# The column stage of a spectral filter beside a gated MLP: the column transform's step is dealt first in every gap, in ten gaps with three rests

## The chip, the cores and the metric

One core of a Trainium2 chip runs the whole kernel. The metric is the device time of one execution in microseconds (us); the kernel before takes 1312.53 us, the median of three runs (1312.05 to 1313.11). The core's engines are named as in its profile: PE is the matrix engine (PEld its weight loads), DVE the vector engine, ACT the scalar engine, POOL and SP mostly issue DMAs. Each takes its own instructions in the order in which the program lists them.

## The reference, cut to what matters

```python
def _A_ref(x, w_r, w_i):                       # x: 1 x 2048 x 576, float32
    X = jnp.fft.rfft2(x, axes=(-2, -1))
    X = X * (w_r + 1j * w_i)
    return jnp.fft.irfft2(X, s=(S, D), axes=(-2, -1))
def _B_ref(x, w_gate, w_up, w_down):           # 576 -> 4608 -> 576
    g, u = x @ w_gate, x @ w_up
    return (gelu(g) * u) @ w_down
g = sigmoid((x * gate_w).sum(-1, keepdims=True))
return g * _A_ref(A_x, A_w_r, A_w_i) + (1 - g) * _B_ref(A_x, w_gate, w_up, w_down)
```

Both branches read the same 2048 x 576 input.

## The kernel before, in words

**The MLP is PE's work and sets the order.** Float32 products are made of fp32r high and low parts. After two ordinary blocks the hidden layer is computed in 34 *groups* (`products`), each one a Strassen-like product of two hidden tiles and two blocks of 512 tokens: seven block products named a11, a12, s2, s3, s1, a22 and s4, each made of two *sevens* (`Block.seven`: seven 128x512 matmuls, lines 1399 and 1401, into the PSUM buffers `px` or `pgu`). Behind each pair of sevens stands a *down* (`down`, line 978: twelve 128x288 matmuls of the down projection into one of two `pdn` buffers); behind the last pair stand two. So a group has 14 sevens and 8 downs. Between them the other engines prepare weights (`Block.prep`: ACT copies the high part, DVE takes the low part, line 1383, and a DMA brings the tail, line 1375), copy PSUM tiles out, apply the GELU and multiply.

**Gaps.** Behind each seven and each down stands a *gap* (`gap`, `dealt`), 22 in a group. There the program first lists what is due by count (`at(n, fn)`: n gaps later), and then takes instructions from the spectral branch, a chain of Python generators in `gens`. A generator's `yield c` says that it has listed c us of DVE work; `yield None` ends its share of this gap. A number `credit` is raised by each matmul's time and lowered by DVE work; it is capped (`cap`, 2.4 in the column stage), and the generators are asked for more only while it is above zero.

**The spectral branch** runs on DVE, ACT and DMA beside the MLP: row transforms, then the *column stage* (`columns`), then the inverse row transforms. The column stage has two chains:

- The *column transform*: 16 steps `kb`. A step makes a first product from `xh`, `xl` (`product(0, ...)`, line 351: six 128x290 matmuls into a `pdn` buffer), copies it out (`zr`, `t0`), combines it on DVE (lines 432 and 433), turns it by two half copies on ACT (`turned`, lines 250 and 251), multiplies by the filter's weights `w0`, `w1` (lines 443, 444), adds (450 to 452) and splits the sum into a high part `yh` and a low part `yl` (431), from which the next step makes the second product, for column kb - 1; that one is copied back to a tile in `rows`. `xl` for the next step is line 457. The weights of the next step come by DMA on SP (line 341).
- The *chain beside it* (`beside`, held in `side`): butterflies and twiddles over four tiles (`column_four`, lines 259 and 266; `column_twiddles`, line 283), stores of finished tiles to `home` and loads of new ones from `away` (line 308, on SP). A backward part waits until the transform has four new tiles (`done`), the transform waits for a forward part (`made`).

In the kernel before, `dealt` asks the chain beside first while `ahead` is set, and then, if credit is left, the transform. A step takes at least eight gaps and more where the credit was used up. A down's result is copied out by ACT (line 1011) in the gap behind it (`post`).

Two PSUM buffers `pdn` serve downs and column products in turn, so a product or a down must wait until the one before the last has been copied out.

Of the kernel before, what the change touches and what calls it, by code (L numbers as in the profile page):

```python
# [27 lines left out]
ROWS = 5120  # L28
UNIT = ROWS // 4
RATE = 1.08  # L30
STEP = 8
FIRST = 2
APART = (13, 14, 16, 17)
PAIRS = ((2, 3, 4, 5), (6, 7, 8, 9), (10, 11, 12, 13), (14, 15, 16, 17), (0, 1))
# [126 lines left out]
def _build(nc, tc, a):  # L161
    with ExitStack() as ctx:
# [8 lines left out]
        def f(x):  # L171
            return x.bitcast(F32)
# [62 lines left out]
        def copy(o, i):  # L235
            act.activation(o, i, AF.Copy)  # L236
# [6 lines left out]
        def two(x):  # L243
            return x.rearrange("p (c k) -> p c k", c=2)[:, :, 0:NK]
# [3 lines left out]
        def turned(o, x, s):  # L248

            act.activation(o[0:64], x[64:128], AF.Copy, scale=-s)  # L250
            act.activation(o[64:128], x[0:64], AF.Copy, scale=s)
# [38 lines left out]
        def columns():  # L290
# [9 lines left out]
            def tile_of(kb):  # L300
                return G[kb // 4 % 2][kb % 4]
# [37 lines left out]
            def load_ww(kb, c):  # L339
                if kb < 16:  # L340
                    nc.sync.dma_start((w0, w1)[c], a["wf"][turn[kb], c])

            def step(us=0.0):
                credit[0] -= us
                yield None

            def product(d, kb, h, l):
                v = ps_dn()
                for al in range(2):
                    for n, (q, x) in enumerate(((0, h), (1, h), (0, l))):  # L350
                        pe.matmul(v[:, al, :NK], cc[d][2 * al + q], two(x)[:, al], start=n == 0, stop=n == 2)  # L351
                tick(6 * 0.135)
                at(1, lambda: load_cc(d, kb + 1))
                return v
# [66 lines left out]
            for kb in range(16):  # L421
                was, more = kb > 0, kb + 1 < 16
                v = product(0, kb, xh, xl)
                if was:
                    copy(yh, vs)
                yield from step()
                copy(zr, v[:, 1, :NK])
                copy(t0, v[:, 0, :NK])
                yield from step()
                if was:  # L430
                    vec.tensor_tensor(yl, vs, f(yh), ALU.subtract)
                vec.tensor_tensor(zi, t0, zr, ALU.subtract)
                vec.tensor_tensor(zr, t0, zr, ALU.add)
                yield from step(1.67 if was else 0.91)
                while post:
                    post.pop(0)()
                turned(vs, z, 1.0)
                u = product(1, kb - 1, yh, yl) if was else None
                yield from step()
                if was:  # L440
                    copy(two(tile_of(kb - 1)), u[:, :, :NK])
                    done[0] = kb - 1
                vec.tensor_tensor(z, z, w0, ALU.mult)
                vec.tensor_tensor(vs, vs, w1, ALU.mult)
                yield from step(1.52)
                if more:
                    while made[0] < (kb + 1) // 4:
                        yield None
                    copy(xh, tile_of(kb + 1))
                vec.tensor_tensor(z, z, vs, ALU.add)  # L450
                vec.tensor_tensor(vs2[:, 0], zr, zi, ALU.add)
                vec.tensor_tensor(vs2[:, 1], zr, zi, ALU.subtract)
                at(1, lambda kb=kb: load_ww(kb + 1, 0))
                at(2, lambda kb=kb: load_ww(kb + 1, 1))
                yield from step(1.67)
                if more:
                    vec.tensor_tensor(xl, tile_of(kb + 1), f(xh), ALU.subtract)
                yield from step(0.76)
                yield from waits(STEP - 7)
            copy(yh, vs)  # L460
            yield None
            vec.tensor_tensor(yl, vs, f(yh), ALU.subtract)
# [133 lines left out]
        def waits(n):  # L596
            for _ in range(n):
                yield None
# [145 lines left out]
        def spectral():  # L744
            nc.sync.dma_start(free_low[:, SW:SW + D], a["gw"][0:1, :].to_broadcast([P, D]))
            yield from send_away(0, lambda: load_rows(1))
            yield from waits(3)
            yield from other_gates()
            yield from forward_rows()
            yield from send_away(1, other_quads)  # L750
            stage_two = columns()
            ops["go"] = lambda: next(stage_two)
            yield from other_operands()
            yield from stage_two
            for h in range(2):
                yield from inverse_rows(h)
# [7 lines left out]
        gens = []  # L764
        side = []
        credit = [0.0]
# [7 lines left out]
        def at(n, fn):  # L774

            if n == 0:
                fn()
                return
            later.append((count[0] + n, fn))
            later.sort(key=lambda x: x[0])  # L780

        def gap():

            dealt()
            while post:
                post.pop(0)()

        def dealt():

            count[0] += 1  # L790
            while later and later[0][0] <= count[0]:
                later.pop(0)[1]()
            if aux:
                aux.pop(0)()
            credit[0] = min(credit[0], cap[0])
            if not gens:
                return
            ahead = side and ops.get("ahead")
            while ahead and credit[0] > 0:
                v = next(side[0], None)  # L800
                if v is None:
                    break
                credit[0] -= v
            while credit[0] > 0:
                try:
                    v = next(gens[0])
                except StopIteration:
                    gens.pop(0)
                    v = None
                if v is None:  # L810
                    while side and not ahead and credit[0] > 0:
                        v = next(side[0], None)
                        if v is None:
                            break
                        credit[0] -= v
                    return
                credit[0] -= v
# [247 lines left out]
        ops = {}  # L1065
# [201 lines left out]
        def tail_piece(n, raw_t=raw_t, high_t=high_t):  # L1267

            def load():
                for q, o in enumerate((raw_t[:, 0:2], raw_t[:, 3:7:3])):  # L1270
                    nc.sync.dma_start(o, a["wt"][n // 2, n % 2, q].rearrange("p (b k) -> p b k", b=2))

            def total():
                for o, p, q in ((4, 3, 0), (2, 6, 4), (3, 6, 3), (5, 1, 2)):
                    vec.tensor_tensor(raw_t[:, o], raw_t[:, p], raw_t[:, q], ALU.subtract)
                credit[0] -= 1.15

            def high():
                copy(high_t, raw_t)

            def rest():
                vec.tensor_tensor(fr(raw_t), raw_t, f(high_t), ALU.subtract)
                credit[0] -= 1.1

            def store():
                d = tails_d[n // 2].rearrange("(r p) (m c k) -> r p c m k", r=4, m=7, c=2)
                for r, x in enumerate((f(high_t), raw_t, f(high_t), raw_t)):
                    nc.sync.dma_start(d[r, :, n % 2], x)
                stored[n // 2] = n % 2

            return load, total, high, rest, store
# [116 lines left out]
        def products(b, k):  # L1408
# [4 lines left out]
            made = {}  # L1413
            opening, end, turn = k == 0, k == len(b.groups) - 1, (p, i) == (0, NBLK - 1)
            if opening:
                at(6, lambda: credit.__setitem__(0, credit[0] - 2.0))
                for q in range(2 * len(PAIRS) - 2):
                    t = (free_low[:, 0:7 * P] if q % 2 == 0 else wtb[:, 0:7 * P]).rearrange("p (m k) -> p m k", m=7)
                    for n, fn in zip((-4, 6, 8, 9, 10), tail_piece(q + 2, t)):
                        at(max(1, n + 12 * q), fn)  # L1420
# [219 lines left out]
        for k in range(len(b.groups)):  # L1640
            if k == len(b.groups) - 1:
                assert ops["half"]
            products(b, k)
# [63 lines left out]
```

## Time and profile before

| | |
|---|---|
| median of three runs | 1312.53 us (1312.05 to 1313.11) |
| profiled execution | 1312.65 us |
| its span | 1310.9 us |
| matmuls on PE, weight loads | 7210, 7210 |
| DVE, ACT, POOL busy share | 87%, 63%, 23% |
| first and last column product begin (us of the span) | 558.2, 855.5 |
| column products (six matmuls each) | 32 |
| DMA moved | 285.94 MB |

A time inside the span is counted from the span's start. [...] In a timeline row, `x6` merges six instructions that follow each other, and the bracket at the end gives the engine's idle time before the row and what ended it.

### The profile page before, as it was taken

What the parts mean: (1) busy time and instruction counts of PE and PEld (TensorE: products, weight loads), DVE (VectorE), ACT (ScalarE), POOL (GpSimd) and SP (SyncE); (2) the same over time, 40 slices, a digit from 0 to 9 for tenths busy, and PEclk for the clock granted to TensorE, in tenths of its full rate; (3) what the DMA queues carried; (4) which work ended last, traced back from release to release, by engine and by line L of the source; (5) the groups of instructions that cost most, each with busy time, mean ns of one, the idle gap of its engine ahead of it and who ended that gap; (6) DMA issues with size and microseconds to landing.
All of it is one profiled execution on the core that took longest, in us unless ns stands there. A gap on an engine that the chain in (4) does not pass through costs nothing.

```text
span 1310.9 us, 20543 instructions
## 1 busy us (share of the span) xinstructions
PE 1299.9 (99%) x7210; PEld 1150.1 (88%) x7210; DVE 1134.5 (87%) x1734; ACT 831.6 (63%) x1405; POOL 307.7 (23%) x392
## 2 busy tenths in 40 slices
PE   9999999999999999999999999999999999999998
PEld 7888888888888888888888888888888888888888
DVE  7899999988999998778888878778999977999954
ACT  5665655657565667678687878766555566565552
POOL 0011212122221211124321333333331231212151
PEclk9999999999999999999999999999999999999999
DMA  9779999897777799969988999999997798877797
GB/s 350 240 204 235 263 257 244 190 286 138 138 145 146 143 320 367 296 174 272 398 250 202 217 258 222 252 224 209 176 184 152 140 217 206 182 158 141 150 188 194
DMA packets 202537, 285.94 MB, mean 218 GB/s; under 512 B 18177, under 2 KB 118657, under 8 KB 201665
## 3 DMA queue, kind: packets, MB, share of 16 engines
q0 software_dynamic: 64848, 110.13, 49.4%
q1 hardware_dynamic: 137152, 174.06, 40.9%
q8 instruction: 56, 0.92, 0.3%
q10 hardware_dynamic: 432, 0.44, 0.1%
q14 instruction: 49, 0.39, 0.1%
HBM read 157.87 MB, written 137.88 MB: 226 GB/s over the span
## 4 chain that ended last, share of the span: by engine, by line
PE 86%; DMA 5%; DVE 4%; ACT 3%; issue 1%; SPq 1%; DVEq 0%; ACTq 0%
PE pdn L978 31%; PE px L1399 22%; PE pgu L1399 22%; PE px L1401 4%; PE pgu L1401 4%; DMA gub<-tails 1%; PE pdn L351 1%; DMA ye<-stg 1%; DMA gub<-ws 1%; DMA home<-rows 1%; ACT gub L236 0%; DMA tmp<-rows 0%; ACT stg L1011 0%; DMA low<-wgu 0%; DVE gub L1383 0%
## 5 line engine op out<-in xcount | busy, mean ns | idle before, releaser
L1011 ACT ACTIVATE stg<-pdn,omg 128x576 f32<-128x576 f32 x276 | 204.6, 741 | 328.8 <-PE pdn L978 182.5
L993 POOL DMA_DIRECT2D yd<-stg x232 | 202.1, 871 | 778.4 <-ACT stg L1011 752.6
L978 PE MATMUL pdn<-dn,hb 128*128 128x288 f32 x1356 | 199.9, 294 | 1.6 <-ACT rows L236 1.4
L978 PEld LDWEIGHTS pdn<-dn,hb 128*128 128x128 f32 x1356 | 191.7, 188 | 10.7 <-ACT rows L236 2.1
L1399 PE MATMUL pgu<-xhi,gub 128*128 128x512 f32 x480 | 149.0, 392 | 0.0
L1399 PE MATMUL pgu<-til,gub 128*128 128x512 f32 x516 | 132.1, 391 | 1.0 <-ACT xraw L236 1.0
L978 PEld LDWEIGHTS pdn<-dn,ext 128*128 128x128 f32 x816 | 122.2, 188 | 9.3
L978 PE MATMUL pdn<-dn,ext 128*128 128x288 f32 x816 | 129.3, 294 | 0.0
L978 PE MATMUL pdn<-dn,gub 128*128 128x288 f32 x816 | 129.3, 294 | 0.0
L1383 DVE TENSOR_TENSOR gub<-low,gub 128x512 fp32r<-128x512 f32 x151 | 103.4, 685 | 17.5 <-ACT gub L236 15.6
L978 PEld LDWEIGHTS pdn<-dn,gub 128*128 128x128 f32 x816 | 115.4, 188 | 0.0
L1399 PEld LDWEIGHTS pgu<-til,gub 128*128 128x128 f32 x516 | 94.4, 188 | 19.1 <-ACT xraw L236 1.2
L236 ACT ACTIVATE gub<-low 128x512 fp32r<-128x512 f32 (+1 forms) x163 | 100.7, 619 | 12.3 <-DMA low<-wgu 6.1
L1399 PE MATMUL px<-xhi,gub 128*128 128x512 f32 x344 | 106.9, 392 | 1.2 <-DVE gl L1427 0.7
L1399 PE MATMUL px<-til,gub 128*128 128x512 f32 x396 | 101.2, 391 | 0.0
L1399 PEld LDWEIGHTS pgu<-xhi,gub 128*128 128x128 f32 x480 | 86.6, 188 | 14.6
L1399 PE MATMUL pgu<-xlo,gub 128*128 128x512 f32 x240 | 93.6, 390 | 0.0
L1399 PEld LDWEIGHTS px<-til,gub 128*128 128x128 f32 x396 | 72.5, 188 | 13.7
L1399 PEld LDWEIGHTS px<-xhi,gub 128*128 128x128 f32 x344 | 62.0, 188 | 12.3 <-DVE gl L1427 1.2
L978 PE MATMUL pdn<-dn,hx 128*128 128x288 f32 x444 | 70.3, 294 | 0.0
L1401 PE MATMUL pgu<-til,gub 128*128 128x512 f32 x172 | 67.1, 390 | 0.4 <-DMA gub<-tails 0.4
L1399 PE MATMUL px<-xlo,gub 128*128 128x512 f32 x172 | 67.1, 390 | 0.0
(311 smaller groups left out, 2758.6 us busy)
## 6 DMA issues: line engine op xcount, KB each, us to landing
yd<-stg POOLq DMA_DIRECT2D x232, 288.0 KB, 5.4
low<-ws SPq DMA_DIRECT2D x114, 256.0 KB, 5.4
gub<-tails SPq DMA_DIRECT2D x179, 128.0 KB, 4.9
gub<-wd SPq DMA_DIRECT2D x68, 288.0 KB, 5.4
tails<-wtb SPq DMA_DIRECT2D x28, 448.0 KB, 5.6
ye<-stg POOLq DMA_DIRECT2D x32, 288.0 KB, 5.5
yd<-ye POOLq DMA_DIRECT2D x32, 288.0 KB, 7.4
slot<-tails SPq DMA_DIRECT2D x59, 128.0 KB, 4.6
```

Of the source, the lines that this page charges most:

```text
L236: act.activation(o, i, AF.Copy)
L351: pe.matmul(v[:, al, :NK], cc[d][2 * al + q], two(x)[:, al], start=n == 0, stop=n == 2)
L978: pe.matmul(ps[half], h[:, l, c], d[:, q, half * HD:(half + 1) * HD], start=part == 0 and n == 0, stop=part == 1 and n == 2)
L993: pl.dma_start(yd[u], o, accum_op=ALU.add)
L1011: out = lambda: put(u, lambda o: act.activation(o.rearrange("p (c k) -> p c k", c=2), v[:, :, 0:HD], AF.Copy, scale=omg[:, u:u + 1]), i == ...
L1383: vec.tensor_tensor(v[:, 0:5:4], x, f(v[:, 1:4:2]), ALU.subtract)
L1399: pe.matmul(ps, l, x[:, t], start=first and t == 0 and q == 0, stop=False, skip_group_check=True)
L1401: pe.matmul(ps, w[:, 512 + P * s:512 + P * (s + 1)], xt, start=False, stop=True, skip_group_check=True)
```

## The change

In `dealt`, while `ahead` is set and the chain beside is alive, the transform is asked for exactly one share in each gap, whatever the credit; the chain beside is then asked while credit is above zero, and nothing else happens in that gap. A step gets three rests (`yield None`): between the butterfly and the half copies with the second product, between that product's copy and the weight multiplications, and at the end, where it had one before. A step therefore has ten gaps. And in the first group a second debit of 1.5 us of credit is taken, four gaps behind the one of 2.0 us. No instruction of an engine's arithmetic is added or removed, apart from how repeated copies merge; what changes is where each stands among the others.

```diff
-STEP = 8
@@ columns
                 yield from step(1.67 if was else 0.91)
+                yield None
                 while post:
                     post.pop(0)()
                 turned(vs, z, 1.0)
                 u = product(1, kb - 1, yh, yl) if was else None
                 yield from step()
                 if was:
                     copy(two(tile_of(kb - 1)), u[:, :, :NK])
                     done[0] = kb - 1
+                yield None
                 vec.tensor_tensor(z, z, w0, ALU.mult)
...
                     vec.tensor_tensor(xl, tile_of(kb + 1), f(xh), ALU.subtract)
                 yield from step(0.76)
-                yield from waits(STEP - 7)
+                yield None
@@ dealt
-            ahead = side and ops.get("ahead")
-            while ahead and credit[0] > 0:
-                v = next(side[0], None)
-                if v is None:
-                    break
-                credit[0] -= v
+            if side and ops.get("ahead"):
+                credit[0] -= next(gens[0]) or 0.0
+                while side and credit[0] > 0:
+                    v = next(side[0], None)
+                    if v is None:
+                        break
+                    credit[0] -= v
+                return
             while credit[0] > 0:
...
-                    while side and not ahead and credit[0] > 0:
+                    while side and credit[0] > 0:
@@ products
             if opening:
-                at(6, lambda: credit.__setitem__(0, credit[0] - 2.0))
+                for n, us in ((6, 2.0), (10, 1.5)):
+                    at(n, lambda us=us: credit.__setitem__(0, credit[0] - us))
```

Where things stand now is told by the order of the instructions. In the kernel after the change a line that is compared has moved by one to four numbers (978 is 981, 351 is 350, 431 to 433 are 430 to 432, 443 and 444 are 444 and 445, 457 is 458, 963 is 966).

On PE, at the sixth second product (the one for column 5, made in the seventh step); before, it stands behind the last seven of a group:

```order
L1401 MATMUL pgu<-xtl_68,gub_73 128x512
L351 MATMUL pdn<-tmp 128x290 x3
L351 MATMUL pdn<-tmp,gub_73 128x290 x3
L978 MATMUL pdn<-dn,hb_79 128x288 x6
L978 MATMUL pdn<-dn,hx 128x288 x6
L978 MATMUL pdn<-dn,hb_79 128x288 x6
L978 MATMUL pdn<-dn,hx 128x288 x6
L1399 MATMUL px_6401<-xhi_63,slot 128x512 x2
```

and with the change the sixth second product stands behind the first pair of sevens of the next group:

```order
L1404 MATMUL px_6380<-til_334,slot 128x512
L350 MATMUL pdn<-tmp 128x290 x3
L350 MATMUL pdn<-tmp,gub_73 128x290 x3
L981 MATMUL pdn<-dn,hb_79 128x288 x6
L981 MATMUL pdn<-dn,hx 128x288 x6
L1402 MATMUL px_6379<-xhi_63,gub_72 128x512 x2
```

Behind the product there was a down and then another down; now there is one down and then a seven.

On DVE, at the butterfly of the eleventh step (`yl`, `zi` and `zr`, whose `wtb` is what ACT turns); this step's second product keeps its place on PE in front of two downs. Before:

```order
L1364 TENSOR_TENSOR low<-low 128x512
L1383 TENSOR_TENSOR gub_73<-gub_822,gub_73 128x2x256
L1427 TENSOR_TENSOR gl_82<-gl_82,px_6775 128x512
L431 TENSOR_TENSOR tmp<-wtb,tmp 128x580
L432 TENSOR_TENSOR wtb<-rows,wtb 128x290
L433 TENSOR_TENSOR wtb<-rows,wtb 128x290
L1368 TENSOR_TENSOR low<-low 128x512
```

and with the change:

```order
L430 TENSOR_TENSOR tmp<-wtb,tmp 128x580
L431 TENSOR_TENSOR wtb<-rows,wtb 128x290
L432 TENSOR_TENSOR wtb<-rows,wtb 128x290
L1367 TENSOR_TENSOR low<-low 128x512
L1386 TENSOR_TENSOR gub_73<-gub_822,gub_73 128x2x256
L1431 TENSOR_TENSOR gl_82<-gl_82,px_6764 128x512
L1371 TENSOR_TENSOR low<-low 128x512
```

Three instructions of the MLP that stood ahead of the butterfly now stand behind it.

On DVE, from the weight multiplications of the thirteenth step to the low part `xl` for the fourteenth; before:

```order
L443 TENSOR_TENSOR wtb<-wtb 128x580
L444 TENSOR_TENSOR wtb<-wtb,gub_822 128x580
L1383 TENSOR_TENSOR gub_73<-low,gub_73 128x2x256
L1364 TENSOR_TENSOR gub_822<-low,gub_822 128x512
L450 TENSOR_TENSOR wtb<-wtb 128x580
L451 TENSOR_TENSOR wtb<-wtb 128x290
L452 TENSOR_TENSOR wtb<-wtb 128x290
L963 TENSOR_TENSOR ext<-gl_82,ext 128x512
L1427 TENSOR_TENSOR xraw<-xraw 128x512
L259 TENSOR_TENSOR low<-rows 128x580
L259 TENSOR_TENSOR rows<-rows 128x580 x3
L457 TENSOR_TENSOR tmp<-rows,tmp 128x580
```

and with the change, from the addition of a seven ahead of them:

```order
L1448 TENSOR_TENSOR xraw<-xraw,px_7376 128x512
L444 TENSOR_TENSOR wtb<-wtb 128x580
L445 TENSOR_TENSOR wtb<-wtb,gub_822 128x580
L258 TENSOR_TENSOR low<-rows 128x580
L258 TENSOR_TENSOR rows<-rows 128x580 x3
L1448 TENSOR_TENSOR xraw<-xraw,px_7377 128x512
L451 TENSOR_TENSOR wtb<-wtb 128x580
L452 TENSOR_TENSOR wtb<-wtb 128x290
L453 TENSOR_TENSOR wtb<-wtb 128x290
L966 TENSOR_TENSOR gub_73<-xraw,gub_73 128x512
L458 TENSOR_TENSOR tmp<-rows,tmp 128x580
```

The four additions of `column_four` (line 259 before, 258 now) stood behind the three additions of the step (450 to 452) and now stand ahead of them, directly behind the weight multiplications. In the fifth and the ninth step they moved in the same way. On PE the first product that uses this `xl` stood ten gaps behind the second product of the thirteenth step, and now stands six gaps behind it, as in every step. The order also shows that the stage's last product stands one gap earlier than before, the first three gaps later, and that the debit in the first group leaves DVE's first 109 rows as they were; behind these, some instructions of the row transforms stand a gap or more later.

## The prediction

> **What bounds the kernel now.** First the page's head and its table of engines, for what is busy all the time:
>
> ```profile
> span 1310.9 us, 20543 instructions
> PE 1299.9 (99%) x7210; PEld 1150.1 (88%) x7210; DVE 1134.5 (87%) x1734; ACT 831.6 (63%) x1405; POOL 307.7 (23%) x392
> ```
>
> PE is busy for all but 11 us, and the change neither adds nor removes a matmul: it can only win back time in which PE was held up. So the next view is the table of windows, over the column stage and over one group behind it (the columns are busy times of PE, PEld, DVE, ACT and POOL, then granted clock, DMA share and GB/s):
>
> ```profile
> 553.57:937.21 383.64, 379.24 (x2135) 336.38 (x2134) 314.65 (x495) 282.19 (x472) 121.06 (x165) 1.00 0.98 240
> 937.21:972.22 35.01, 35.01 (x196) 31.02 (x196) 34.87 (x43) 18.85 (x31) 11.22 (x12) 1.00 1.03 183
> ```
>
> The windows are cut where the same down of a group begins: ten groups, then one. The undisturbed group takes 35.01 us (196 matmuls, 22 blocks, so 1.59 a block) at a granted clock of 1.00 in both. Ten such groups are 350.1; the first window has 2135 − 1960 = 175 more matmul records, of the column products' 192. A product runs .80 from start to start where nothing holds it up (783.13 to 783.93, below), so 32 are 25.6. 383.64 − 350.1 − 25.6 = **7.9 us lost** in the stage and just behind it. That is about all the change can win there. The view of waits, PE alone over that window, names some of it (us in total, times, longest):
>
> ```profile
> PE pdn L978 <- ACT rows L236: 1.4, 3, 0.5
> PE pgu L1399 <- ACT xraw L236: 1.0, 1, 1.0
> PE px L1399 <- DVE gl L1427: 0.7, 1, 0.7
> PE px L1399 <- ACT pgu L236: 0.5, 1, 0.5
> PE pgu L1401 <- DMA gub<-tails: 0.4, 1, 0.4
> PE pdn L351 <- DVE tmp L457: 0.2, 1, 0.2
> ```
>
> **What the change removes.** The timeline about one of the three waits for `rows`:
>
> ```profile
> 745.97 0.46 DVE L433 TENSOR_TENSOR wtb<-rows,wtb 128x290 f32<-128x290 f32 x1
> 746.52 0.69 ACT L250 ACTIVATE wtb<-wtb 64x580 f32<-64x580 f32 x1 [2.17 <-DVE wtb L433]
> 747.70 0.95 PE L978 MATMUL pdn<-dn,hx 128*128 128x288 f32 x6
> 748.48 0.64 ACT L236 ACTIVATE rows<-pdn 128x580 f32<-128x580 f32 x1
> 749.16 1.06 PE L978 MATMUL pdn<-dn,hb 128*128 128x288 f32 x6 [0.51 <-ACT rows L236]
> ```
>
> The second product (L351, just ahead on PE) stood before two downs. The second down needs the product's PSUM buffer; ACT copies it out only behind the half copies, and these wait 2.17 for the butterfly. From 747.70 to 749.16 are 1.46 where six matmuls take .79 (787.12 to 788.70 for twelve, below), so .67 lost, and .11 more as the restarted six last 1.06 instead of .95: the bracket and .27. The view of waits has three of them, 1.4 together: 1.4 + 3 × .27 = **2.2**. In the new order two of the three steps have one down and then a seven behind the product. The third, the eleventh step, keeps its place, but its butterfly stands ahead of three MLP instructions (.60 each from start to start): 1.8 earlier covers a wait of .5. I take all 2.2.
>
> A product between two downs costs less:
>
> ```profile
> 783.13 0.96 PE L351 MATMUL pdn<-tmp,xtl 128*128 128x290 f32 x6
> 787.12 1.74 PE L978 MATMUL pdn<-dn,hb 128*128 128x288 f32 x12
> 789.10 0.57 PE L351 MATMUL pdn<-tmp,gub 128*128 128x290 f32 x3
> 789.74 1.86 PE L978 MATMUL pdn<-dn,hb 128*128 128x288 f32 x12
> 631.92 0.57 PE L351 MATMUL pdn<-tmp,gub 128*128 128x290 f32 x3
> 632.56 1.73 PE L978 MATMUL pdn<-dn,hb 128*128 128x288 f32 x11
> ```
>
> From 789.10 to 789.74 are .64 where three matmuls take .40 (788.70 to 789.10), and the down lasts .12 longer: .36; at 632 about as much. No second product stands so now: **.7**.
>
> Then `xl` that came late, and a chain through ACT and DMA:
>
> ```profile
> 740.27 1.21 PE L351 MATMUL pdn<-tmp,xtl 128*128 128x290 f32 x6
> 820.77 0.79 PE L351 MATMUL pdn<-tmp,xtl 128*128 128x290 f32 x4 [0.20 <-DVE tmp L457]
> 761.23 0.69 ACT L250 ACTIVATE low<-rows 64x580 f32<-64x580 f32 x1 [1.47 <-DMA rows<-away]
> 767.94 1.67 PE L1399 MATMUL pgu<-til,gub 128*128 128x512 f32 x6 [0.99 <-ACT xraw L236]
> 770.05 0.50 PE L1401 MATMUL pgu<-til,gub 128*128 128x512 f32 x1 [0.44 <-DMA gub<-tails]
> ```
>
> The product at 740 lasts .25 longer than the one at 783; the one at 820 loses .20 + .27: **.7**. At 761 ACT waited 1.47 for a tile of `rows`, with the copies of PSUM queued behind that half copy; six us later a seven (767.94) waited .99 for such a copy and then .44 for a tail: .99 + .44 + 2 × .27 = **2.0**. The tiles, steps and half copies all stand elsewhere now, so I count the old losses as gone, 5.6 in all, and price what comes in their place.
>
> **What it adds.** In the new order credit is read before the step runs, so the step's own debits are overwritten; the chain beside it then finds the full 2.4 us and is taken in a burst. The four additions (old line 259) stand between weight multiplications and `xl` in the fifth, ninth and thirteenth step, six gaps ahead of the product that needs it rather than ten. DVE's timeline of the thirteenth step:
>
> ```profile
> 787.39 0.68 DVE L1444 TENSOR_TENSOR xraw<-xraw,px 128x512 f32<-128x512 f32 x1
> ...
> 791.13 0.76 DVE L443 TENSOR_TENSOR wtb<-wtb 128x580 f32<-128x580 f32 x1 [0.32 <-ACT wtb L251]
> 791.81 0.76 DVE L444 TENSOR_TENSOR wtb<-wtb,gub 128x580 f32<-128x580 f32 x1
> 792.49 0.68 DVE L1383 TENSOR_TENSOR gub<-low,gub 128x512 fp32r<-128x512 f32 x1
> 793.09 0.68 DVE L1364 TENSOR_TENSOR gub<-low,gub 128x512 f32<-128x512 f32 x1
> 793.69 0.75 DVE L450 TENSOR_TENSOR wtb<-wtb 128x580 f32<-128x580 f32 x1
> 795.23 0.68 DVE L963 TENSOR_TENSOR ext<-gl,ext 128x512 fp32r<-128x512 f32 x1
> 796.43 0.75 DVE L259 TENSOR_TENSOR low<-rows 128x580 f32<-128x580 f32 x1
> 799.57 0.76 DVE L457 TENSOR_TENSOR tmp<-rows,tmp 128x580 fp32r<-128x580 f32 x1
> ```
>
> From start to start: two multiplications 1.36 (791.13 to 792.49), a 512-wide instruction .60, 450 to 452 1.54 (793.69 to 795.23), the four additions 3.14 (796.43 to 799.57). The new rows are one seven's addition, the multiplications, the four, another addition, 450 to 452, one more and `xl`: .60 + 1.36 + 3.14 + .60 + 1.54 + .60 + .76 = 8.60. That first addition can begin only when its seven has ended, and five blocks later (5 × 1.59 = 7.95) the product wants `xl`: late by .65 with DVE free, and by up to 2.4 with DVE arriving 1.9 behind, as before (the addition at 787.39 was for the seven behind the product of 783.13, which ended at 783.13 + .80 + 1.59 = 785.5). In the fifth step the rows from the multiplications on add up to the same 8.60, against five blocks and some .3 of lead: .4, up to 1.7. In the ninth three 512-wide ones less, 6.8: .2, up to 1.1. DVE got a free stretch ahead of the multiplications in all three by the order, so I take values near the lower ends, .9, .4 and .2: **+1.5** (0 to 5.2).
>
> ACT's half copies (.69, as at 746.52) now stand four together three times, once for the step and once for the chain beside: 2.8 in a block of 1.59, with PSUM copies behind them. The nearest row of such a meeting, the one behind 761, cost 1.3 for the copy alone; without a wait for DMA ACT has the time (282 busy of 384 us). I take **+.7** (0 to 1.3 at each of two places).
>
> The tiles' loads from `away` are issued two gaps earlier and used three gaps earlier.
>
> ```profile
> 750.26 1.36 SPq L308 DMA_DIRECT2D rows<-away  x2
> DMA to landing us min/median/max: 5.0/7.8/10.2
> ...
> L250 ACT ACTIVATE low<-rows 64x580 f32<-64x580 f32 x21 | 14.4, 688 | 6.3 <-DVE rows L259 4.4 <-DMA rows<-away 1.5
> ```
>
> ACT wanted the tile at 759.76, 9.5 after issue; it will want it 1.6 sooner, at 7.9. A load of the median still lands in time, one as slow as the last costs 1.47 + 1.6 = 3.1 of ACT, and PE about .5 more. Nearest is the median, since the group of all 21 such half copies shows 1.5 for this DMA, the one wait at 761: **+.8** (0 to 3.6; 6.2 of ACT if the earlier issue doesn't bring an earlier landing, all DMA engines being busy .98). [...]
>
> Behind the stage DVE, late from two waits for DMA, holds PE up twice:
>
> ```profile
> 905.91 0.73 PE L1399 MATMUL px<-xhi,gub 128*128 128x512 f32 x2 [0.72 <-DVE gl L1427]
> 909.86 0.72 PE L1399 MATMUL px<-xhi,gub 128*128 128x512 f32 x2 [0.47 <-ACT pgu L236]
> ```
>
> .72 + .47 + 2 × .27 = 1.7. All of the inverse row transforms stand a gap (1.6) earlier, which about covers the larger; I take **−1.0** (0 to −1.7, and above nothing if the earlier order meets other MLP work).
>
> The second debit in the first group costs nothing by the order. PE's one wait near it (.51 at 85.64, for a `slot`) ends on DVE's 96th row, and the order changes only from the 110th. Behind that PE waits for nothing up to the stage, and rows a gap later don't alter that.
>
> **The sum**, against the profiled execution's 1312.65 (the median is 1312.53): −5.6 + 1.5 + .7 + .8 − 1.0 = −3.6, so 1309.05. From the median that is 1308.9; I say **1309.0**.
>
> **The rivals.**
>
> *Nothing new comes late.* For it: PE's stalls shrink as products meet fewer pairs of downs, and ACT and DVE are not full in the stage (282 and 315 of 384). Against it: 8.60 against 7.95. It gives 1312.65 − 5.6 − 1.0 = 1306.0.
>
> *DVE comes late into the bursts.* For it: DVE arrived 1.9 late at that place before. Then the terms of `xl` are 5.2 instead of 1.5, and the sum −5.6 + 5.2 + .7 + .8 − 1.0 = +.1: 1312.7, no change.
>
> *Slower: ACT is held at the tile from `away`.* DMA is saturated, and a load asked for earlier lands no earlier; then ACT waits up to 6.2 at a half copy, with the copies of PSUM behind it, in the last two sets. PE loses the wait and about .5. At a mean of 4.7 (between 3.1 and 6.2) two sets cost 10.4, in place of .8: −3.6 − .8 + 10.4 = +6.0, 1318.6. It decides from a loss of 4.4 at the loads on (slower than before), 7.0 for past the bound. Against it: the group of half copies has one such wait in the whole stage.
>
> *The change doesn't do what it says.* The step's debits are lost, as told; this is in the order already and so in the sum. The debit in the first group alone would be 0, 1312.5.
>
> **How the numbers follow.** A measurement of this kernel tells .2% (2.6 us) from no change: faster means under 1309.9. The forecast has .48 with 1306.9 to 1311.3 for its own spread (the terms .9 + .4 + .2 and .7 each between nothing and double, the loads to 3.6): .33 of it faster, .15 same. Nothing late: .15, faster. DVE late: .27, same. ACT held: .10, slower. So faster .48, same .42, slower .10. The range leaves out the slower rival and the edges: 1305.6 to 1313.2.
>
> **What would show it.** In the profile after: no wait of a down for `rows` in the stage (else the first term is wrong); PE's waits for `tmp` from the line of `xl` just ahead of the products of the sixth, tenth and fourteenth steps, the last the longest, .4 to 1.2 (none: the first rival; over 1.5 each: the second); at ACT's first half copies of a tile, a wait for `rows<-away` under 3.6 in one set (two sets over 4: the third); the waits at 906 and 910 shorter. An undisturbed group must again take 35.01. The prediction is wrong if PE loses time at a place that this text doesn't name, such as before the stage, where the debit moves row transforms.

## The result and the profile after

The changed kernel takes 1320.62 us (median of 6 runs, 1319.40 to 1321.79), the kernel before 1312.60 in the same runs: a ratio of 1.006, interval 1.0047 to 1.0073. That is 8 us slower, where 1309.0 was forecast and the range ended at 1313.2. Of all the runs below, one stands apart, 3351 us among e3's ten; no record says why, and its ratio leaves it out.

The page's head and engines of the changed kernel's profile, and the windows between the same two downs of the program as before (553.57 to 937.21 there) with the group behind them:

```profile
span 1318.7 us, 20567 instructions
PE 1303.3 (99%) x7210; PEld 1153.2 (87%) x7210; DVE 1135.1 (86%) x1734; ACT 830.0 (63%) x1405; POOL 307.5 (23%) x392
...
554.47:944.84 390.37, 381.88 (x2135) 338.61 (x2134) 316.87 (x496) 281.49 (x472) 121.16 (x165) 0.99 0.96 237
944.84:979.86 35.02, 35.02 (x197) 31.03 (x196) 34.88 (x45) 18.84 (x31) 11.20 (x12) 1.00 1.05 183
```

An undisturbed group takes 35.02 as before, and DVE and ACT are as busy in us as they were. The stretch takes 390.37 instead of 383.64, and its first down begins .90 later. So 6.7 of the 7.8 us that the span grew are lost in the column stage, and .9 ahead of it. Against the prediction's 375.7 (350.1 for ten groups and 25.6 for 32 products) the stage now loses **14.7 us instead of 7.9**. PE's waits (us in total, times, longest):

```profile
PE pgu L1402 <- ACT xraw L235: 3.5, 3, 2.3
PE pdn L350 <- DVE tmp L458: 3.0, 2, 2.6
PE px L1402 <- ACT xraw L235: 2.0, 1, 2.0
PE pgu L1554 <- DVE gate L1550: 1.5, 1, 1.5
PE px L1402 <- DVE gl L1431: 0.6, 1, 0.6
PE pdn L350 <- DVE tmp L430: 0.2, 1, 0.2
```

No down waits for `rows` any more (1.4 before). Five places took its room. PE's rows overlap (six 128x288 matmuls at 628.21 last .95, and the next row begins .79 behind), so a loss is taken from start to start against the undisturbed pace: 2.9 us at 616, .6 at 692, 4.6 from 767 to 778, .7 at 800 and 3.9 from 813 to 820, 12.7 in all in the stage; 1.1 at 325, ahead of it; 1.2 at 913 and 917, behind it (1.7 before).

**At 616** a product of the fourth step waits for `xl`. The timelines of DVE and ACT, and PE's row:

```profile
608.45 0.69 ACT L250 ACTIVATE low<-rows 64x580 f32<-64x580 f32 x1
609.16 0.76 DVE L282 SCALAR_TENSOR_TENSOR rows<-rows,low 128x580 f32<-128x580 f32 x1 [4.12 <-ACT low L250]
617.95 0.76 DVE L458 TENSOR_TENSOR tmp<-rows,tmp 128x580 fp32r<-128x580 f32 x1
618.76 0.80 PE L350 MATMUL pdn<-tmp,xtl 128*128 128x290 f32 x4 [2.60 <-DVE tmp L458]
```

DVE stood still for 4.12 us at an addition of the chain beside (L282, the third twiddle). What it waited for is a half copy on ACT that ends at 609.14, and that had queued there behind a PSUM copy and the step's own half copies. All of DVE's work for `xl` stood behind that addition.

**From 767 to 778** the two engines wait for each other in turn:

```profile
762.66 0.76 DVE L282 SCALAR_TENSOR_TENSOR rows<-rows,low 128x580 f32<-128x580 f32 x1 [3.52 <-ACT low L250]
766.21 0.69 DVE L966 TENSOR_TENSOR hb<-xraw,hb 128x512 fp32r<-128x512 f32 x1
767.01 0.60 ACT L235 ACTIVATE xraw<-pgu 128x512 f32<-128x512 f32 x1 [2.00 <-DVE hb L966]
769.74 0.63 ACT L235 ACTIVATE gub<-gub 128x512 fp32r<-128x512 f32 x1 [2.13 <-DVE gub L1367]
772.51 0.68 ACT L250 ACTIVATE low<-rows 64x580 f32<-64x580 f32 x1
773.22 0.60 ACT L235 ACTIVATE xraw<-pgu 128x512 f32<-128x512 f32 x1
773.87 2.29 PE L1402 MATMUL pgu<-til,gub 128*128 128x512 f32 x6 [2.26 <-ACT xraw L235]
```

DVE waits 3.52 for ACT at the same kind of addition, then has three of the chain's four additions ahead of the MLP's L966, and the step's butterfly and the fourth ahead of its L1367; ACT, its PSUM copies queued, waits 2.00 and 2.13 for these two; then four half copies stand ahead of the copy that PE needs. **At 813** ACT is only full. The window from the first of eight half copies to the copy that PE waits for:

```profile
805.63:814.49 8.86, 7.50 (x46) 6.64 (x44) 7.12 (x12) 8.62 (x14) 3.37 (x5) 1.00 0.99 179
```

ACT is busy 8.62 of 8.86, 5.5 of it with the eight half copies (.69 each), and the PSUM copy comes 2.0 late. Behind both places PE itself runs at half speed, a granted clock of .50 for 3.41 us (last section).

### The profile page after: what moved, and what is told of

Read it like the earlier page. It is cut to its first block, busy times and chain, and to the rows that moved or that the text cites. A ratio compares the mean times of both kernels' runs of the same rounds, so it can differ in the third digit from the quotient of the medians.

```text
span 1318.7 us, 20567 instructions
## 1 busy us (share of the span) xinstructions
PE 1303.3 (99%) x7210; PEld 1153.2 (87%) x7210; DVE 1135.1 (86%) x1734; ACT 830.0 (63%) x1405; POOL 307.5 (23%) x392
## 4 chain that ended last, share of the span: by engine, by line
PE 85%; DVE 6%; ACT 4%; DMA 3%; issue 1%; SPq 0%; DVEq 0%; ACTq 0%
PE pdn L981 29%; PE px L1402 22%; PE pgu L1402 21%; PE px L1404 4%; PE pgu L1404 3%; PE pdn L350 1%; DMA away<-tmp 1%; DMA rows<-away 1%; DVE rows L258 1%; PE px L917 1%; ACT tmp L740 1%; ACT low L249 1%; ACT low L250 1%; ACT stg L1014 1%; PE pgu L917 0%
## 5 line engine op out<-in xcount | busy, mean ns | idle before, releaser
L1402 PEld LDWEIGHTS pgu<-xhi,gub 128*128 128x128 f32 x480 | 86.6, 188 | 14.7
```

Source lines behind the costliest of these rows:

```text
L1402: pe.matmul(ps, l, x[:, t], start=first and t == 0 and q == 0, stop=False, skip_group_check=True)
```

## The experiments

Times are medians, each with the 95% interval of its ratio to the kernel before in the same job. The stage's loss is what it was above; "ahead" is where the first of the two downs begins (553.57 before), "behind" the time from the end of the group behind the stage to the last matmul's start (333.7 before).

| run | time, us | ratio's interval | ahead | stage loses | behind |
|---|---|---|---|---|---|
| changed kernel | 1320.62 | 1.0047–1.0073 | 554.5 | 14.7 | 333.7 |
| e12, the same again | 1321.16 | 1.0044–1.0083 | 554.9 | 16.8 | 333.7 |
| e1, debits kept | 1317.82 | 1.0032–1.0062 | 555.3 | 6.9 | 337.5 |
| e2, one opening debit | 1316.55 | 1.0025–1.0051 | 553.2 | 12.1 | 333.7 |
| e3, before + second debit | 1314.45 | 1.0005–1.0025 | 554.5 | 9.6 | 333.7 |
| e4, before + rests | 1342.66 | 1.0225–1.0262 | 553.1 | 9.0 | 363.2 |
| e5, chain beside first | 1322.31 | 1.0060–1.0091 | 554.6 | 17.1 | 333.7 |
| e6, two to a gap | 1311.84 | 0.9987–1.0006 | 555.8 | 4.6 | 333.7 |
| e7, seven tenths kept, one debit | 1317.17 | 1.0021–1.0049 | 553.6 | 12.1 | 333.7 |
| e8, debits kept, one debit | 1315.86 | 1.0013–1.0044 | 553.6 | 7.0 | 335.3 |
| e9, rest in the twiddles | **1308.68** | 0.9958–0.9980 | 554.0 | 3.0 | 334.1 |
| e10, e6 and e9 | 1309.41 | 0.9967–0.9986 | 553.4 | 3.4 | 334.9 |
| e11, e6 with one debit | 1311.73 | 0.9986–1.0004 | 553.7 | 7.2 | 333.7 |
| e13, two empty gaps | 1316.01 | 1.0012–1.0031 | 558.0 | 9.7 | 333.7 |
| e14, before + e9's rest | 1312.56 | 0.9986–1.0005 | 554.0 | 7.4 | 334.2 |
| e15, e9 with one debit | 1314.56 | 1.0003–1.0022 | 554.3 | 10.7 | 333.7 |

The stage's loss is read from one profile of each kernel. Two profiles of the changed kernel, the first row and e12, differ by 2.1, of which 1.5 stand at 616, where the granted clock fell to .50 in e12 alone (last section). So a difference of two us between two losses may be chance.

**First set: which part of the change costs.**

e1, on the changed kernel:

```diff
-                credit[0] -= next(gens[0]) or 0.0
+                us = next(gens[0]) or 0.0
+                credit[0] -= us
```

> The changed kernel with one statement split in two, so that the step's own debits (6.4 us a step by its numbers) are kept and the chain beside it gets only what is left. Theory A (the chain beside is dealt in bursts because the step's debits are lost, and DVE and ACT then wait for each other inside a burst): the long waits of PE for xl at 616 (2.6 us) and for the PSUM copies at 771 and 812 (2.3 and 2.0) go, with the slow matmuls behind them; the time falls by 6 to 10 us, to 1310.5 to 1314.5. Theory B (the fixed ten gaps, with products at new places, are to blame): the products stand at the same ten gaps, so the waits stay and the time is 1318 or more.

The stage loses 6.9, 7.8 less, and less than in the kernel before. But the time, for which A had a fall of 6 to 10, fell by 2.8, since the chain beside now gets too little and the steps wait for its tiles: the stage ends 16 gaps later, and the last downs wait for DVE's final sums (L1052), whose operand the inverse rows store late. And the wait at 616, which A had going, stayed (2.2). Its view of waits; the third row lies at 713, a place that the changed kernel doesn't have:

```profile
PE pdn L350 <- DVE tmp L458: 2.9, 2, 2.2
PE pdn L982 <- DVE low L1052: 2.0, 1, 2.0
PE pdn L982 <- ACT stg L1015: 1.7, 1, 1.7
```

e2 (`for n, us in ((6, 2.0),):`, so one debit):

> The changed kernel with only the one old debit in the first group. Theory A (the second debit moves the row transforms so that one PSUM copy at 325 comes late, 1.1 us, and relieves the wait at 85, .7 us): the wait at 325 goes and the one at 85 comes back; the time changes by -0.4, so 1320.2. Theory B (the wait at 325 comes from the column stage's new order, or is chance): the wait at 325 stays; 1320.6 to 1321.3.

The wait at 325 is gone, as A has it; the one at 85 did not come back (.3 lost), and the gain is 4 us, not .4: the stage begins three gaps earlier, its waits stand at other places, and it loses 2.6 less.

e3, the kernel before with the two debits of the changed kernel:

> The kernel before with the second debit in the first group and nothing else. Theory A: a PSUM copy late at 325 (+1.1), the wait at 85 gone (-.7), the column stage as before or shifted by a gap: 1313.0. Theory B (the debit does nothing): 1312.6. If the column stage's start moves to another gap, all its meetings change, and the time may lie 3 us to either side.

2 us slower, above A and B and within the 3 us allowed for a stage that moves: no wait at 325, one for a tail at 291 (1.1), and, with the stage six gaps later, waits of products for their coefficients that the kernel before hasn't:

```profile
PE pdn L351 <- DMA xtl<-col: 3.8, 2, 2.6
```

e4, the kernel before with the three rests, and no new dealing:

> The kernel before with the three rests and without the new dealing (the chain beside is still asked first and all debits count). Theory A (bursts are what costs): no PE wait over 1 us in the column stage and no slow matmuls; the stage is some 30 gaps longer, and second products stand elsewhere; 1308 to 1313. Theory B (the rests cost, by moving the products): over 1316.

30 us slower, but by neither theory's cause. The stage loses 9.0, 7.4 of it at one wait of 5.4 and the slow matmuls behind it (a granted clock of .53 from 805.0 to 808.0); its end moved 43 gaps back, and the last downs wait for the same sums:

```profile
PE pdn L980 <- DVE low L1050: 26.1, 1, 26.1
PE px L1401 <- ACT xraw L236: 5.4, 1, 5.4
```

So the rests need the new dealing, which keeps a step at ten gaps; and a stage that ends 13 to 16 gaps later than the changed kernel's has a price at the end (1.6 us in e8, 3.7 in e1).

**Second set: depth or order of a burst.**

e5 puts the loop over `side` ahead of `credit[0] -= next(gens[0]) or 0.0`:

> The changed kernel, with the chain beside asked ahead of the transform's share in each gap again; the step's debits stay lost, so the bursts stay as deep. Theory A1 (what costs is that the chain's half copies and additions stand behind the step's within a gap): the wait of 2.6 us at 616 goes, the stage loses 9 us or less instead of 14.7, and the time is 1315 or less. Theory A2 (the depth of a burst costs, whichever chain comes first): the stage loses 12 to 16 us, 1318 to 1322.

A1 is wrong on the time: 616 falls to .3, but other waits come (2.8 at 687, 1.5 at 744, 2.8 at 771), and the stage loses 17.1, more than A2's 12 to 16.

e6, on the changed kernel:

```diff
+                taken = 0
-                while side and credit[0] > 0:
+                while side and credit[0] > 0 and taken < 2:
+                    taken += 1
```

> The changed kernel, with the chain beside giving at most two DVE instructions to a gap instead of up to four; products stay at the same gaps up to the thirteenth step, and the stage ends five gaps later. Theory A2 (depth): the stage loses 7 to 10 us instead of 14.7, no wait for xl over 1.5 us; 1313 to 1316, with the second debit's 1 us ahead of the stage still in it. Theory B (the products' new places cost): 1319 to 1322.

Better than A2 had it: 4.6, of which 2.9 are still at 616. The one at 767 is gone, with the products at the same gaps up to the twelfth step, in which it lay; so theory B, that the products' new places cost, is out for it. The later steps stand five gaps later here, which leaves the place at 813 open until e13.

e7 replaces the statement of e1 by one that keeps seven tenths of the step's debits, with one debit in the first group; e8 is e1 with one debit:

> The changed kernel with seven tenths of the step's debits kept and only the old debit in the first group; the stage ends four gaps later than in the changed kernel. Theory A2: bursts are shallower, the stage loses 7 to 9 us, nothing is lost ahead of it (325 or 291) and less than 1 us at the end: 1311.5 to 1314. Theory B: 1317 or more.

> The changed kernel with all of the step's debits kept and only the old debit in the first group: the first run of this study without the second debit. Its column stage ends at gap 526 instead of 529. If the wait for a tail at 291 (1.4 us) came from the second debit, it goes, and the wait at the end (2.0) shrinks by the three gaps: 1312.5 to 1315. If the wait at 291 is a matter of DMA alone, it stays and the time is 1316 to 1318.

e8 loses 7.0 in the stage, as e1; the wait at 291 is gone, and the end's is shorter; its time is a little above the 1315 expected, and its ten runs lie from 1312.9 to 1322.3. e7 missed: the stage loses 12.1, and the time lies where B had it. Its largest wait (4.4) comes from what the prediction's third rival named, ACT held at a tile from `away`. ACT's and DVE's rows there:

```profile
769.48 0.69 ACT L249 ACTIVATE low<-rows 64x580 f32<-64x580 f32 x1 [7.27 <-DMA rows<-away]
...
770.91 0.76 DVE L282 SCALAR_TENSOR_TENSOR rows<-rows,low 128x580 f32<-128x580 f32 x1 [7.21 <-ACT low L250]
```

**Third set: the addition behind the half copies.**

e9, on the changed kernel, in `column_twiddles`:

```diff
                 else:
+                    if o == 3:
+                        yield None
                     vec.scalar_tensor_tensor(x, x, c, t, op0=ALU.mult, op1=ALU.add)
```

> The changed kernel with one more rest in the chain beside it, between the half copies of the third twiddle and the addition that needs them. Theory A3 (the wait at 616 is DVE standing 4.1 us at that addition, behind half copies that were listed in the same gap and queue on ACT): the wait at 616 falls under 0.5 us and the time by 2 to 3.5 us, to 1317 to 1318.5; the waits at 771 and 812 may change, since the stage ends two gaps later. If DVE's wait at that addition stays over 3 us, A3 is wrong and the time is 1320 or more.

12 us faster than the changed kernel, 4 faster than the one before, and the best of all. At 616 A3 is borne out only in part (DVE's wait there 2.92 instead of 4.12, PE's 1.5 instead of 2.6, where under .5 was expected). More came at 762, where DVE's wait was 3.52 and now ACT and PE run on, and at 813, where PE's wait is gone; neither was forecast. The rows of this kernel:

```profile
761.98 0.76 DVE L284 SCALAR_TENSOR_TENSOR rows<-rows,low 128x580 f32<-128x580 f32 x1 [0.47 <-ACT low L250]
763.37 0.60 ACT L235 ACTIVATE xraw<-pgu 128x512 f32<-128x512 f32 x1 [0.17 <-PE pgu L1406]
768.77 1.52 PE L1404 MATMUL pgu<-til,gub 128*128 128x512 f32 x6
```

> The changed kernel with both: at most two DVE instructions of the chain beside to a gap, and the rest ahead of the third twiddle's addition. Products stand at the same gaps as with the limit of two alone (1311.8). Theory A2 and A3: the stage loses 1.5 to 3 us instead of 4.6, the time is 1308 to 1310.5, faster than the kernel before. Rival (the wait at 616 only moves to the next product): 1311 to 1313.

The time is in the range of A2 and A3, the stage's loss a little above it, and both together are not better than the rest alone: 3.4, with 1.8 still at 616.

> The changed kernel with at most two DVE instructions of the chain beside to a gap and only the old debit in the first group; the stage begins three gaps earlier than with both debits, so every product stands beside other MLP work. If the second debit's only effect is the loss ahead of the stage (2.2 us by that run's record: 555.8 against 553.6), the time is 1309 to 1310. If the placing of the stage against the groups decides as well (DVE's work by the listed order is bunched more in it), the stage loses 7 to 11 us and the time is 1312 to 1316.

The time lies between the two expectations, the stage's loss in the second: ahead 2.1 are saved, in the stage 2.6 given back.

> The changed kernel again, unaltered, for a second profile. If the waits are set by the listed order, those at 616, 771 and 812 (PE waiting 2.6, 2.3 and 2.0 us) are found again within 0.5 us each, and the time is 1319 to 1322. If they hang on when transfers land, they differ by over 1 us or stand elsewhere.

The waits are set by the listed order: 2.59 at 616, 2.26 at 773 and 2.00 at 815.

**Fourth set: the rest or the shift.** The rest moves the last five steps back by two gaps. e13 makes that shift alone (`if kb == 11: yield from waits(2)`):

> The changed kernel with two empty gaps in the twelfth step, so that its products stand at the same gaps as with the rest in the twiddles, and without that rest. Theory A3 (the rest itself, by keeping DVE off half copies of the same gap, took the 12 us): the waits at 616 (2.6) and at 771 (2.3 with slow matmuls behind) stay, those behind the twelfth step may change; 1314 to 1321. Theory C (the last five steps' new places took most of it): the stage loses 3 to 6 us; 1309 to 1312.

The waits at 616 and 771 are there again, at 619 and 775, and the one at 813 is not. The third row lies at 292, ahead of the stage:

```profile
PE pgu L1404 <- ACT xraw L235: 2.6, 2, 2.3
PE pdn L350 <- DVE tmp L460: 2.6, 1, 2.6
PE px L1406 <- DMA gub<-tails: 2.2, 1, 2.2
```

The products stand at the same gaps as in e9. By the stage's loss (14.7, 9.7, 3.0) the shift is worth 5.0 of e9's gain and the rest itself 6.7; the times say the same (4.6 and 7.3). A3 and C each have a part.

> The kernel before with the rest ahead of the third twiddle's addition and nothing else. Theory A3 with its limit (before, that addition's waits of 11.5 us in all sat where xl was not next): little to win, 1310.5 to 1313. If the rest is worth as much by itself as in the changed kernel: under 1306.

The time is as before, but as the sum of a gain and a loss. DVE's waits at the line of the twiddles' additions fell from 11.5 to 2.2, and PE's losses at 740, 749, 820, 906 and 910, 3.2 in all, are gone. In their place ACT stands for a tile from `away`, and PE loses 4.6 from 767 to 773, where it lost 2.0 before:

```profile
765.03 0.68 ACT L250 ACTIVATE low<-rows 64x580 f32<-64x580 f32 x1 [5.35 <-DMA rows<-away]
767.24 1.06 PE L980 MATMUL pdn<-dn,ext 128*128 128x288 f32 x6 [2.44 <-ACT stg L1013]
```

So this run doesn't show that the addition cost nothing in the old dealing.

> The changed kernel with the rest in the twiddles and only the old debit in the first group; the stage begins three gaps earlier. If the second debit costs by what it does ahead of the stage (about half a us in the profile with the rest): 1307.5 to 1308.5. If the stage's place against the groups counts more, as with the limit of two (stage loss 7.2 against 4.6): 1310 to 1313.

Slower than either expectation: as in e11, the stage three gaps earlier loses more (10.7 against 3.0) than the debit does ahead.

## Why the prediction was wrong

**What bounds the kernel**, and the old stalls: right. All of it is PE's waits, nearly all in the stage, and the stalls counted as gone (5.6) are gone: no down waits for `rows`, none of the old chain at 761 to 770.

**The term that failed is ACT's half copies**, "+.7 (0 to 1.3 at each of two places)". It measured 4.6 and 3.9 at two places. Some 1.6 and 1.5 of these (an estimate: the 3.39 us from 774.44 had a granted clock of .53, the 3.10 from 815.50 one of .52) are matmuls at half speed behind the wait, which the sum had nowhere. The step said "without a wait for DMA ACT has the time (282 busy of 384 us)". That is a share of the stage, and it says nothing of one place: with the step's debits lost, the chain beside lists its half copies and the additions that need them in one share, behind the step's half copies. At 762 DVE waits 3.52 for ACT, then ACT 4.1 for DVE, and PE's PSUM copy is behind both; at 813 eight half copies nearly in a row are enough. e1, which keeps the debits (and has its later steps elsewhere), e6, which limits the depth of a burst, and e9, which parts the half copies from their addition, each take the first away, and e13, with e9's gaps and without its rest, has it again. The second goes with a shift of the last steps by two gaps (e13); that ACT's eight half copies made it is read from the rows, and no run took them alone away.

**The term of `xl`** had the right sum of DVE work and the wrong list of places. At the fourteenth step's product it is .7 where .9 was expected; at the sixth and tenth it is nothing (.4 and .2 expected). The fourth step, 2.9, was left out, since the term added up DVE's durations and no wait inside them: the 4.12 of L282 is the price. The groups of the line of the twiddles' additions in the kernel before, the changed one and e9, over the stage:

```profile
L283 DVE SCALAR_TENSOR_TENSOR rows<-rows,low 128x580 f32<-128x580 f32 x13 | 9.9, 760 | 11.5 <-ACT low L251 11.5
```

```profile
L282 DVE SCALAR_TENSOR_TENSOR rows<-rows,low 128x580 f32<-128x580 f32 x13 | 9.9, 760 | 14.6 <-ACT low L250 14.6
```

```profile
L284 DVE SCALAR_TENSOR_TENSOR rows<-rows,low 128x580 f32<-128x580 f32 x13 | 9.9, 759 | 9.0 <-ACT low L250 9.0
```

The kernel before already had 11.5 us of such waits. They weren't weighed, since PE didn't wait behind them. Their sum alone doesn't tell the price: it is 17.2 in e1, whose stage loses 6.9, and 4.6 in e10, whose stage loses 3.4. What counts is whether PE's next operand stands behind one of them.

**The loads** (+.8) cost nothing here: no wait for `away` in this profile. In e7, e4 and e14 a tile from `away` holds ACT for 7.3, 6.6 and 5.4, with PSUM copies behind it, so what that rival feared can happen, but it did in other orders. The 16 loads, issued on SP, landed after 4.8 to 9.1 in this profile, 6.2 in the median.

**Behind the stage** −1.0 was forecast and −.6 came (1.2 lost, 1.7 before).

**The second debit** was priced at nothing "by the order", with PE's waits ahead of the stage looked for only in the old trace. It moves the row transforms: of nine profiles with two debits eight show a wait of .4 to 2.2 at 291 or 325 (of a PSUM copy behind DVE, or of a tail), of eight with one none does. It also begins the stage three gaps later, which changed the stage's loss by +2.6 in the changed kernel (against e2), by −.1 with the step's debits kept (e1 against e8), and by −2.6 and −7.6 with the limit of two and with the rest (e6 against e11, e9 against e15). The 2.6 are near what two profiles of one kernel differ by. By the times the debit costs 4.1 and 2.0, then nothing, and in e9 it saves 5.9, so the sign of its whole price hangs on the rest of the order.

**The rival on the other side** came near the measured time (1318.6) by luck. At 767 it was right in kind, ACT held with PSUM copies queued, and wrong in what holds it: DVE, not a DMA. At 813 nothing holds ACT; it is full.

**Slips in the working** changed nothing of this. A group has 194 matmuls (14 sevens of 7, 8 downs of 12), and the 196 of the window count two that reach in from its ends, so no record of a product is missing. With DVE 1.9 behind, .65 late becomes some 2.5, not 2.4. And the forecast's spread up to 1311.3 leaves out the loads' 3.6 that its words count in; with them it ends at 1314.1.

Open is why the stage's place against the groups matters as it does. The runs show that it can, by up to 7.6 us (e9 against e15), and no run took it apart.

## What to carry to other kernels

Where two engines serve each other, look at each pair "copy on one, use on the other" that is listed in one share: ahead of 616 all of DVE's work stood still for 4.12 us for what was ahead of the copy on ACT, and ACT's busy time over the stage, 281 of 390 us, did not show it. A wait in the old trace that costs nothing, like the 11.5 us here, can cost in a new order, so list such waits by size before moving anything. Parting the pair by a rest was worth 6.7 us of the stage's loss in this dealing, and nothing on the whole in the old one. In an augmented assignment whose right side changes the same variable, the old value is read first: where a scheduler's budget is lowered inside the call, the debit is lost.

## What the runs showed of the hardware

PE ran at half speed behind some of its waits. In the changed kernel's trace two such stretches stand in the stage. They begin at 774.66 and 815.62, each has a granted clock of .50 for 3.41 us, and they are 40.96 apart, which is twelve times 3.413. In e4, about the wait of 5.4 and behind it, the mean clock was .72 from 798.5 to 804.0 and .53 from 805.0 to 808.0, some 5.9 us at half speed in the two (an estimate from these means). The windows below are 3.413 long; those of the changed kernel lie whole multiples of that ahead of its two stretches, and those of e12, e8 and e14 are cut for each profile by itself. The first number behind the comma is PE's busy time, and the last three columns are granted clock, DMA share and GB/s. The changed kernel, at 616 and at 773:

```profile
614.23:617.65 3.42, 1.94 (x15) 1.69 (x13) 3.38 (x7) 0.12 (x1) 1.25 (x3) 1.00 1.11 401
617.65:621.06 3.41, 2.30 (x12) 2.01 (x13) 3.13 (x5) 3.36 (x7) 0.00 (x0) 1.00 1.05 412
771.25:774.66 3.41, 1.15 (x5) 0.67 (x4) 1.39 (x2) 3.34 (x6) 2.89 (x4) 1.00 0.87 173
774.66:778.07 3.41, 3.41 (x13) 3.00 (x11) 3.38 (x6) 2.93 (x6) 1.45 (x2) 0.50 1.24 215
```

The same kernel in e12, at 616; then e8 and e14, two cases close to each other:

```profile
616.06:619.48 3.42, 0.83 (x6) 0.58 (x6) 3.14 (x7) 1.51 (x3) 0.54 (x1) 1.00 1.12 401
619.48:622.89 3.41, 3.41 (x11) 2.83 (x10) 3.34 (x5) 3.41 (x6) 0.44 (x1) 0.50 1.04 407
```

```profile
632.04:635.45 3.41, 1.50 (x9) 1.26 (x10) 3.41 (x7) 2.58 (x5) 0.60 (x2) 1.00 1.04 406
635.45:638.86 3.41, 3.41 (x13) 3.13 (x12) 3.09 (x6) 1.64 (x4) 2.08 (x5) 0.50 1.03 408
```

```profile
765.44:768.85 3.41, 1.61 (x12) 1.61 (x12) 0.22 (x1) 3.30 (x6) 1.55 (x3) 1.00 1.12 300
768.85:772.26 3.41, 2.16 (x9) 1.25 (x8) 3.00 (x5) 3.34 (x7) 1.51 (x3) 1.00 1.20 215
```

In these rows a window at full clock in which PE was busy for .83, 1.15 or 1.50 us was followed by one at .50, and a window with 1.61 or 1.94 was not. The changed kernel's window from 812.21 to 815.62, with 1.42, was followed by .50 too. So the closest two are some 1.9 us without a matmul (3.41 − 1.50, in e8), with half speed behind them, and 1.8 (3.41 − 1.61, in e14), without.

The waits at 616 are 2.60 and 2.59 long. In the first execution a window begins inside the wait, at 617.65, and the clock stays; in e12 the whole wait lies in the window from 616.06 to 619.48, and the next runs at .50, so that 4.4 us are lost there instead of 2.9. So in these two executions of one kernel the same wait cost 1.5 more where it lay in one window. That its place in the windows made the difference is read from these rows; no run moved that alone.
